# Linear attention and two token mixers on one core: attention products grouped by kind, buffers handed over by the program, one mixing in float32, a new order

## The chip, the core and the metric

The kernel runs on one core of a Trainium2 chip. The core has a matrix engine (TensorE, PE in the rows; its weight loads are shown as PEld), a vector engine (VectorE, DVE), a scalar engine (ScalarE, ACT), a general engine (GpSimd, POOL), and a queue that issues transfers (SyncE, SP). PE writes only into PSUM, which is used here as 8 banks of 128x512 float32. The metric is the device time of one execution in microseconds: 698.87 us before (median of 3 runs, 698.83 to 698.91).

## The reference

Three stages follow each other. Batch is 4, 768 tokens, 8 heads of 48 channels (384 channels in all).

```
# 1. linear attention with a decaying state, per batch and head
state = alpha[t, :, None] * state + outer(k[t], v[t]);   y[t] = q[t] @ state
# 2. first mixer: tokens through rank 32, then channels through 4*384
u  = x + (x.T @ U @ V).T;   x1 = u + relu(u @ w_ch1) @ w_ch2
# 3. second mixer
theta = x1 @ w_theta;  zr, zi = x1*cos(theta), x1*sin(theta)
u  = x1 + w_tok_r @ zr + w_tok_i @ zi;   out = u + relu(u @ w_ch)
```

## The kernel before

**Attention.** A pair of heads (64 partitions each, 48 used) of one batch is one unit of work; there are 16 such pairs, 4 to a batch. The 768 tokens are cut into 6 chunks of 128. `prep_k` and `prep_q` (L189 on, with `scale_k` and `scale_q` from L173 on) run two scans over the decay on VectorE (tiles `G` and `al`) and scale `kk` and `qq` by them; the multiplications are VectorE's for the first pairs and GpSimd's after that, as the strings `BY_K` and `BY_Q` say. `att_pe` (L217) then issues the products of a pair on TensorE, in kinds:

- `kT` (L248): five transposes of `kk`, copied by ScalarE into `kt`.
- `A` (L228): scores of a token half (three chunks, two heads). Each half is masked into two `Am` tiles: for the first four pairs by a copy on ScalarE and a select on GpSimd (L235, L236), for the others by a masked copy on VectorE (L239).
- `D` (L265): what each chunk adds to the state; two of its twelve products multiply zeros. A scan on VectorE (L272, tile `S`) turns it into states.
- `Y`: per half, the product of the masked scores with v (L285) and then that of the states with q (L290), into one bank; ScalarE copies it to `xp` (L292), and transfers carry it into the `X` tiles.

The order within a pair is: `kT`, `A` of half 0, `D`, scan, `A` of half 1, then for each half `Y` of the scores and `Y` of the states. In the trace a float32 product shows as two matmul instructions, so the 6 products of one `A` half are "x12".

**First mixer.** For batch 0, `rank_columns` (L342) works by 128 channels as soon as these are complete: transposes of `X` (L348), a split into a high and a low part (ScalarE L138, VectorE L139), 12 products with U in the reduced format fp32r (L308), and `lift` (L333), which multiplies by V (L335), adds to `X` on VectorE (L337) and splits the sum into `uh`. `expand` and `contract` are the channel products, 9 fp32r products of 384 columns each (L446 to L448), with weights that VectorE puts together from raw bits (`conv`, L376 to L380) and splits (L394). **Second mixer:** `theta`, `mix` (L600) and `chan`, all with such fp32r products.

**What sets the order.** The string `ORDER` names, letter by letter, the generator that is to issue its next piece (A attention, P preparation, D loads, 0 to 2 mixing of batch 0, L weights, M and N the channel products of the two token halves, and so on). Instructions keep that order on each engine. Tiles come from two pools: one tag of 59 slots in SBUF, one of 8 banks in PSUM; the pool gives a slot again when its tile is released.

Of the kernel before, what the change touches and what calls it, by code (L numbers as in the profile page):

```python
# [18 lines left out]
NP = H // 2  # L19
# [10 lines left out]


# [4 lines left out]
AAAPAAQAPAUAUAAUUPAAUAAAPUAAPAAAU00AALLDA0PAQALALALPLA10LAP0A1AAALL1LALAA212AQA22120LAMMLL21MLLLMLM1LLLMNNDMNM  # L36
MLMANLLNLNPNNLMMLLLMLNMLNMMQLLLLLNNMLMMLMMMDMPMPNAAQAQAAADPANAAPAAAAAAPLANAAADAAQPAANQADPNPNKKNNKKKKAAAAAAAPKK
KNAAKKNKQNADAAAAAPNMAAPMMMMQMKMMMMDPQMAAAAAAPQMMDMMAKMMAKMAAAAAAPMPNMNQMNDAMKAMKAAA2APAAMKANKPNNKKNDNKPQNNKNKA
NKAAAAAADPQNNNTPAANKNAAAAAAAPANAAAATAATAKNKMMKMMKMMMMNNKNNNKQMKKNKTNTMMMKMMTQKNNNNLMMMKMKUTNTLKLNNNNNNXMTMKTMT
NNMNMAHNNMKNKKNNHKHTKTNMNNMHHMNMMHMNNTMNLNMMTTNNFMMMMMTMMTTMNMHT0MNHTNNTTTMNTLNMMHNNMNMGTGHTHTNNHHTNHNTNGTGNNX  # L40
TNGTTGHTHHGTTGLTGGGLHGGGHGTGGXGHHGTTHAGHGGGHGGTTTTGGGPTGHHGGGHGHLGHGGGGFGGGGGFCGGHCCGHHHLHGFGDGHHGHMGGHGCGCGGH
NGHGGGGGPGTHHGGGHGGGGHCGGGHHCCGPGGHHHHGGGGHGGLGGHHGHGHGXGGGHHHGHGLG0GGHHGGGGHGCGHCGCHGGHGGGGCGHHGHGGGHGHGGGHGG
HHGGGGHHGHHGLLHGGGGGCGHGCGGGGCHLGGGCGGFGGGGCCCCCCCHCGC
# [4 lines left out]
    "VVVVPPPPPPPPPPPP", "VVVVPPPPPPPPPPPP", "VVVVVVVVVVVV",  # L48
# [12 lines left out]
def linear_attention_moe_kernel(ctx, tc, aT, kT, qT, vP, vT, U, V4, w1, w2, wth, wtr, wti, wch, out):  # L61
# [29 lines left out]

    def T(name, dt=F32):
        return pools["big"].tile([128, 768], dt, tag="s", name=name)

    def PS(name):
        return pools["ps"].tile([128, 512], F32, tag="p", name=name)
# [102 lines left out]
    def prep_q(b, p):  # L199
        if b + p:  # L200
            scale_q(b, p, 0, S)
        a, k, q, v, G = pr.pop((b, p))
        i = b * NP + p
        tt = pools["sml"].tile([128, NC, 1], F32, tag="tt", name="tt")
        tb = pools["sml"].tile([128, D, NC], F32, tag="tb", name="tb", bufs=2)
        dve.tensor_tensor(out=tt[:, 0:NC - 1], in0=v[:, NC * 96 + 1:NC * 97].unsqueeze(2), in1=cols(G, 0)[:, 1:NC],
                          op=ALU.mult)
        dve.memset(tt[:, NC - 1:NC], 0.0)  # L208
        act.copy(tb, tt.rearrange("p c o -> p o c").to_broadcast([128, D, NC]))
# [5 lines left out]
        pr[b, p] = (k, q, v, tb, squares)  # L215

    def att_pe(b, p):  # L217
        k, q, v, tb, squares = pr.pop((b, p))
# [3 lines left out]
        def scores(g):  # L222
# [7 lines left out]
            for h in range(2):  # L230
# [7 lines left out]
                else:  # L238
                    dve.copy_predicated(out=m, mask=maskb, data=t)  # L239
                ms.append(m)  # L240
            return ms

        def across(g):
# [5 lines left out]
            act.copy(k3[:, 3 * g:3 * g + n], t[:, 0:n * 128].rearrange("p (c d) -> p c d", d=128))  # L249

        across(0)
        if b + p:
            across(1)
        yield 750
        ma = scores(0)
        if b + p == 0:
            across(1)
        yield 1280
        late.append(squares)
        dps = PS("D")  # L260
        d3 = dps[:, 0:NC * D].rearrange("p (e c) -> p c e", c=NC)
        for c in range(NC):
            for h in range(2):
                w = v[:, c * 96 + h * D:c * 96 + (h + 1) * D] if c < NC - 1 else zero
                pe.matmul(d3[64 * h:64 * h + 64, c], k3[:, min(c, NC - 2), 64 * h:64 * h + 64], w,  # L265
                          start=True, stop=True)
        yield 800


        st = pools["sml"].tile([128, D, NC], F32, tag="S", name="S", bufs=2)  # L270
        flat = "p e c -> p (e c)"
        dve.tensor_tensor_scan(out=st.rearrange(flat), data0=dps[:, 0:NC * D], data1=tb.rearrange(flat),  # L272
                               initial=0.0, op0=ALU.add, op1=ALU.mult)
        yield
        mb = scores(1)
        yield 1280
        xp = T("xp")
        ms = (ma, mb)
        for g in range(2):
            t = PS("Y")  # L280
            cs = [(3 * g + j, slice(j * C, (j + 1) * C), j) for j in range(3)]
            for c, o, j in cs:
# [4 lines left out]
            for c, o, j in cs:  # L287
# [5 lines left out]
            yield 1500  # L293
        for h in range(2):
            ch = (2 * p + h) * D
            done = 0
            while done < D:
                j, r = divmod(ch + done, 128)
                n = min(D - done, 128 - r)
                sync.dma_start(X[b][j][r:r + n, :], xp[64 * h + done:64 * h + done + n, :])  # L300
                done += n
        yield 100
# [7 lines left out]
    def rank(b):  # L310
        g = PS("g")
        xs = {}
        for s in range(NC + 2):
            if s < NC:
# [4 lines left out]
                split(t[:, 0:384], xs[s][:, 0], xs[s][:, 1])  # L319
            if s > 1:  # L320
                x = xs.pop(s - 2)
                contract_tokens(g[:, 0:384], s - 2, x[:, 0], x[:, 1])
            yield 700
        gt = pools["sml"].tile([128, 384], F32R, tag="gt", name="gt", bufs=1)
        act.copy(gt, g[:, 0:384])
        dve.tensor_tensor(out=gt[96:128], in0=g[96:128, 0:384], in1=gt[96:128].bitcast(F32), op=ALU.subtract)
        yield
        for hf in range(2):
            for j in range(KD):
                lift(b, hf, j, gt[:, j * 128:(j + 1) * 128])  # L330
                yield

    def lift(b, hf, j, g):  # L333
        t = PS("h")
        pe.matmul(t[:, 0:HT], g, uv[1][:, hf * HT:(hf + 1) * HT], start=True, stop=True)  # L335
        x = X[b][j][:, hf * HT:(hf + 1) * HT]
        dve.tensor_tensor(out=x, in0=t[:, 0:HT], in1=x, op=ALU.add)  # L337
        uh = two(T("uh", F32R))
        split(x, uh[:, 0], uh[:, 1], e_hi=act)
        UH[b, hf, j] = uh  # L340

    def rank_columns(b, j):  # L342
        xs = []
        for n in range(2):
# [9 lines left out]
        for n in range(2):  # L354
            for i in range(3):
                s = 3 * n + i
                o = slice(i * 128, (i + 1) * 128)
                contract_tokens(g[:, 0:128], s, xs[n][:, 0, o], xs[n][:, 1, o])
# [3 lines left out]
        dve.tensor_tensor(out=gt[96:128], in0=g[96:128, 0:128], in1=gt[96:128].bitcast(F32), op=ALU.subtract)  # L362
        yield
# [20 lines left out]
    def load_w12():  # L384
# [3 lines left out]
        def put(n, W):  # L388
            def high(v):
# [3 lines left out]
                def low():  # L393
                    (dve if BY_W[n] == "V" else pool).tensor_tensor(out=l, in0=v, in1=h.bitcast(F32), op=ALU.subtract)  # L394
                    W.extend((two(h)[:, i], two(l)[:, i]) for i in range(2))
# [29 lines left out]
    def load_uv():  # L425
# [9 lines left out]
        pool.tensor_tensor(out=a[:, :, 0:RANK], in0=u3, in1=a[:, :, RANK:2 * RANK].bitcast(F32), op=ALU.subtract)  # L435
        v4 = T("v4", F32R)
        act.copy(v4, got[1])
        pool.tensor_tensor(out=v4[32:64], in0=got[1][32:64], in1=v4[32:64].bitcast(F32), op=ALU.subtract)
        yield 0
        uv[:] = [a, v4]  # L440
# [10 lines left out]

    def expand(b, hf, f, uh, pend=pend):
        t = PS("h1")
        for j in range(KD):
# [5 lines left out]
                                 op0=ALU.max, op1=ALU.subtract)  # L460
        pend.append((b, hf, f, h))

    def contract(pend=pend):
# [3 lines left out]
        for j in range(KD):  # L467
            w = [x[:, j * 128:(j + 1) * 128] for x in W2[f]]
            three(acc[b, hf][j][:, 0:HT], w, (h[:, 0], h[:, 1]), f == 0, f == NF - 1)
        if f == NF - 1:  # L470
            for j, t in enumerate(acc.pop((b, hf))):
                x = X[b][j][:, hf * HT:(hf + 1) * HT]
                dve.tensor_tensor(out=x, in0=t[:, 0:HT], in1=x, op=ALU.add)
            ended.append(b)
# [25 lines left out]
    def spill(b):  # L500
        for j in range(KD):
            d = dr.tile([128, 768], F32, name=f"x1d{b}_{j}")
            sync.dma_start(d, X[b][j])
            x1d[b, j] = d
# [5 lines left out]
    def load_second():  # L510
# [3 lines left out]
        def put_thch(v):  # L514
            v = two(v)
            pool.tensor_scalar(out=v[:, 0], in0=v[:, 0], scalar1=INV2PI, scalar2=0.0, op0=ALU.mult, op1=ALU.add)
            for i, W in ((0, TH), (1, CH)):
                t = two(T("wt", F32R))
                split(v[:, i], t[:, 0], t[:, 1], e_lo=by())
                W.append(t)  # L520

# [407 lines left out]
```

## Time and profile before

| | |
|---|---|
| median of 3 runs | 698.87 us |
| profiled execution | 698.41 us, span of its instructions 696.7 us |
| PE busy | 670.8 us (96%), 4818 instructions |
| DVE, ACT, POOL busy | 397.7 (57%), 248.1 (36%), 139.6 (20%) us |
| granted TensorE clock, mean | 0.995 |
| chain of waits | 85% of the span on PE, 6% DVE, 3% issue, 2% DMA, 2% POOL |

The page's busy share is an average over stages. Up to 63.07 us, where the channel products of the first mixer begin, PE has gaps and DVE is the busiest engine; from there to 691.11 us, its last product, PE hardly stops; the last 5.6 us are the final vector operations and the transfers of the result.

### The profile page before, as it was taken

The page shows a single profiled execution, that of the slowest core. Times are in us where ns is not written, and L with a number is a line of the kernel's source. Part 1 is how long each engine was busy: PE and PEld are TensorE (multiplying, and loading weights), DVE is VectorE, ACT ScalarE, POOL GpSimd, SP SyncE. Part 2 cuts the span into 40 slices and gives each one's busy share as a digit, 9 for nine tenths or more (in the row PEclk, how much of TensorE's full clock was granted, in tenths as well). Part 3 has the DMA queues.
Part 4 walks back from the last instruction along what each step waited for, and adds up shares of the span by engine and source line. Part 5 has one row for each costly group of instructions (what it writes and reads, how often), then busy time and mean ns, then how long its engine had stood idle before and what let it go on. Part 6 is the DMA issues. An engine that isn't in the chain of part 4 may idle for free.

```text
span 696.7 us, 11660 instructions
## 1 busy us (share of the span) xinstructions
PE 670.8 (96%) x4818; PEld 640.9 (92%) x4818; DVE 397.7 (57%) x610; ACT 248.1 (36%) x512; POOL 139.6 (20%) x123
## 2 busy tenths in 40 slices
PE   5879999999999999999999999999999999999996
PEld 4658999898888998899999999999999999999996
DVE  7798887686545565435344635667644363344423
ACT  3554332454332433324233323234343243434310
POOL 5440011431321231001121111323440121112010
PEclk9999999999999999999999999999999999999999
DMA  8562656163712233102120311244100000000012
GB/s 311 178 227 64 221 165 193 40 195 103 250 50 78 86 103 109 36 1 113 56 104 1 114 45 47 91 159 158 47 1 35 24 13 22 1 35 12 1 45 97
DMA packets 24078, 63.22 MB, mean 91 GB/s; under 512 B 2896, under 2 KB 6864, under 8 KB 24016
## 3 DMA queue, kind: packets, MB, share of 16 engines
q1 hardware_dynamic: 24016, 62.39, 26.6%
q8 instruction: 40, 0.66, 0.4%
q14 instruction: 22, 0.18, 0.1%
HBM read 49.40 MB, written 8.26 MB: 83 GB/s over the span
## 4 chain that ended last, share of the span: by engine, by line
PE 85%; DVE 6%; issue 3%; DMA 2%; POOL 2%; ACT 1%; SPq 1%; POOLq 0%; ACTq 0%; DVEq 0%
PE mx L600 19%; PE h L446 7%; PE acc L446 7%; PE acc L447 7%; PE h L448 7%; PE h L447 7%; PE acc L448 7%; PE A L228 3%; PE Y L285 3%; PE Y L290 3%; PE ch L448 2%; PE ch L447 2%; PE ch L446 2%; PE th L448 2%; PE th L447 2%
## 5 line engine op out<-in xcount | busy, mean ns | idle before, releaser
L459 DVE SCALAR_TENSOR_TENSOR hh<-h,hh 128x384 fp32r<-128x384 f32 x96 | 52.4, 554 | 103.2 <-ACT hh L458 103.2
L447 PE MATMUL acc<-hh,wh 128*128 128x384 f32 x288 | 96.5, 335 | 1.4 <-DVE hh L459 1.4
L446 PE MATMUL h<-uh,wh 128*128 128x384 f32 x288 | 97.7, 339 | 0.1
L446 PE MATMUL acc<-hh,wh 128*128 128x384 f32 x288 | 97.5, 339 | 0.0
L448 PE MATMUL acc<-hh,wl 128*128 128x384 f32 x288 | 96.5, 335 | 0.0
L448 PE MATMUL h<-uh,wl 128*128 128x384 f32 x288 | 96.5, 335 | 0.0
L447 PE MATMUL h<-uh,wh 128*128 128x384 f32 x288 | 96.4, 335 | 0.0
L458 ACT ACTIVATE hh<-h 128x384 fp32r<-128x384 f32 x96 | 46.0, 489 | 97.2 <-PE h L448 93.3
L600 PE MATMUL mx<-wkh,zh 128*128 128x384 f32 x288 | 74.8, 340 | 0.0
L600 PE MATMUL mx<-wkl,zh 128*128 128x384 f32 x288 | 73.3, 335 | 0.0
L600 PE MATMUL mx<-wkh,zl 128*128 128x384 f32 x288 | 73.2, 335 | 0.0
L447 PEld LDWEIGHTS acc<-hh,wh 128*128 128x128 f32 x288 | 54.1, 188 | 1.7 <-DVE hh L459 1.7
L446 PEld LDWEIGHTS h<-uh,wh 128*128 128x128 f32 x288 | 54.1, 188 | 1.6 <-DVE hh L459 0.7
L446 PEld LDWEIGHTS acc<-hh,wh 128*128 128x128 f32 x288 | 54.1, 188 | 1.1
L448 PEld LDWEIGHTS acc<-hh,wl 128*128 128x128 f32 x288 | 54.1, 188 | 0.1
L447 PEld LDWEIGHTS h<-uh,wh 128*128 128x128 f32 x288 | 54.1, 188 | 0.0
L448 PEld LDWEIGHTS h<-uh,wl 128*128 128x128 f32 x288 | 54.1, 188 | 0.0
L600 PEld LDWEIGHTS mx<-wkh,zl 128*128 128x128 f32 x288 | 52.1, 188 | 0.0
L600 PEld LDWEIGHTS mx<-wkl,zh 128*128 128x128 f32 x288 | 51.9, 188 | 0.0
L600 PEld LDWEIGHTS mx<-wkh,zh 128*128 128x128 f32 x288 | 50.9, 188 | 0.0
L139 POOL TENSOR_TENSOR wkl<-cv,wkh 128x768 fp32r<-128x768 f32 x12 | 22.8, 1901 | 100.4 <-ACT wkh L138 100.4
L187 POOL TENSOR_TENSOR qq<-qq,al 128x768 f32<-128x768 f32 x12 | 23.4, 1952 | 92.4 <-DVE tt L208 50.2
(126 smaller groups left out, 1193.1 us busy)
## 6 DMA issues: line engine op xcount, KB each, us to landing
raw<-in_w SPq DMA_DIRECT2D x12, 768.0 KB, 4.5
al<-in_aT SPq DMA_DIRECT2D x15, 384.0 KB, 3.8
kk<-in_kT SPq DMA_DIRECT2D x15, 384.0 KB, 4.7
qq<-in_qT SPq DMA_DIRECT2D x15, 384.0 KB, 5.1
vv<-in_vP SPq DMA_DIRECT2D x16, 291.0 KB, 5.4
raw<-in_wtr SPq DMA_DIRECT2D x6, 768.0 KB, 4.2
raw<-in_wti SPq DMA_DIRECT2D x6, 768.0 KB, 4.2
out<-ot SPq DMA_DIRECT2D x24, 192.0 KB, 1.9
```

The source lines that it names most:

```text
L139: (e_lo or dve).tensor_tensor(out=lo, in0=src, in1=hi.bitcast(F32), op=ALU.subtract)
L187: (dve if BY_Q[b * NP + p] == "V" else pool).tensor_tensor(out=q[:, o], in0=q[:, o], in1=a[:, o], op=ALU.mult)
L228: pe.matmul(ts[h][:, j * C:(j + 1) * C], k[r, c], q[r, c], start=True, stop=True)
L285: pe.matmul(t[64 * h:64 * h + n, o], v[:, c * 96 + h * D:c * 96 + h * D + n], ms[g][h][:, j], start=(j == 0), stop=(c == 0), skip_group_ch ...
L290: pe.matmul(t[64 * h:64 * h + D, o], st[64 * h:64 * h + 64, :, c - 1], q[64 * h:64 * h + 64, c * C:(c + 1) * C], start=False, stop=True, s ...
L446: pe.matmul(out, a[0], b[0], start=first, stop=False)
L447: pe.matmul(out, a[0], b[1], start=False, stop=False)
L448: pe.matmul(out, a[1], b[0], start=False, stop=last)
L458: act.activation(h[:, 0], t[:, 0:HT], ACTF.Relu)
L459: dve.scalar_tensor_tensor(out=h[:, 1], in0=t[:, 0:HT], scalar=0.0, in1=h[:, 0].bitcast(F32), op0=ALU.max, op1=ALU.subtract)
L600: pe.matmul(ACC[b, j][hf][:, 0:HT], z[:, i, c], w[:, hf * HT:(hf + 1) * HT], start=f, stop=l)
```

## The change

1. `att_pe` with `LATE = 0` issues both halves of a kind together: `kT`, `A` of half 0, `A` of half 1, `D`, the scan, `Y` of the scores for both halves, `Y` of the states for both halves.
2. `D` leaves out its two products with zeros; VectorE writes the zeros into the bank before the scan.
3. Tiles are taken from lists of free slots and banks that the program keeps itself (`take`, `done_with`); each slot has a tag of its own, and the slot that was given back first is taken first.
4. For batch 0 `rank_columns` mixes in float32: `xs` is one plain copy, six products with a float32 tile `uf` take the place of twelve with `ua`. In `lift` (batch 0), a product of the identity with `X` adds `X` in the bank, ScalarE copies the sum back, and the split reads the bank.
5. One pair's `qq` multiplication goes from GpSimd to VectorE (`BY_Q`), squares are noted earlier, X tiles are allocated when first written, and `ORDER` is another string.

```
+LATE = 0
...
-    "VVVVPPPPPPPPPPPP", "VVVVPPPPPPPPPPPP", "VVVVVVVVVVVV",
+    "VVVVPPPPPPPPPPPP", "VVVVPPPVPPPPPPPP", "VVVVVVVVVVVV",
...
+    free, home = {"on": True, "s": list(range(SLOTS)), "p": list(range(8))}, {}
+    def take(kind, name, width, dt):
+        p = pools["big" if kind == "s" else "ps"]
+        if not free["on"]:
+            return p.tile([128, width], dt, tag=kind, name=name)
+        i = free[kind].pop(0)
+        t = p.tile([128, width], dt, tag=f"{kind}{i}", name=name, bufs=1)
+        home[t.tensor.name] = kind, i
+        return t
...
+    def done_with(*ts):
+        for t in ts:
+            if t.tensor.name in home:
+                kind, i = home.pop(t.tensor.name)
+                free[kind].append(i)
...
+        def increments():
+            t = PS("D")
+            d3 = t[:, 0:NC * D].rearrange("p (e c) -> p c e", c=NC)
+            for c in range(NC - 1 if after else NC):
...
+        def states(t):
+            if after:
+                dve.memset(t[:, 0:NC * D].rearrange("p (e c) -> p c e", c=NC)[:, NC - 1], 0.0)
...
+        after = b * NP + p >= LATE
+        across(0)
...
+        ms.append(scores(0))
...
+        if after:
+            yield
+            ms.append(scores(1))
+            done_with(k)
+            yield
+            dps = increments()
+            yield
+            st = states(dps)
+            yield
+            xp = T("xp")
+            ts = [PS("Y") for _ in range(2)]
+            for g in range(2):
+                within(ts[g], g)
...
+            yield
+            for g in range(2):
+                before(ts[g], g)
...
     def lift(b, hf, j, g):
         t = PS("h")
...
+        if b == 0:
+            pe.matmul(t[:, 0:HT], ident, x, start=True, stop=False)
+            pe.matmul(t[:, 0:HT], g, uv[1][:, hf * HT:(hf + 1) * HT], start=False, stop=True)
+            split(t[:, 0:HT], uh[:, 0], uh[:, 1], e_hi=act)
+            act.copy(x, t[:, 0:HT])
+            done_with(t)
+            return
...
     def rank_columns(b, j):
...
-            x = two(T("xs", F32R))
-            split(t[:, 0:384], x[:, 0], x[:, 1])
-            xs.append(x)
+            act.copy(two(xs)[:, n], t[:, 0:384])
...
-                contract_tokens(g[:, 0:128], s, xs[n][:, 0, o], xs[n][:, 1, o])
+            pe.matmul(g[:, 0:128], uv[2][:, o], xs[:, o], start=(s == 0), stop=(s == NC - 1))
...
+        w = T("uf")
+        pool.memset(w, 0.0)
+        act.copy(w.rearrange("p (s n r) -> p s n r", s=NC, n=4)[:, :, 1:4], u3.unsqueeze(2).to_broadcast([128, NC, 3, RANK]))
```

Three places show how instructions stand. First PE, the pair after the first batch (the sixth row of `kT` in the program before): one kind per token half.

```order
L248 MATMUL kT<-ident,kk 128x128 x5
L228 MATMUL A<-qq,kk 128x128 x6
L265 MATMUL D<-vv,kt 64x48 x10
L265 MATMUL D<-zero,kt 64x48 x2
L228 MATMUL A<-qq,kk 128x128 x6
L285 MATMUL Y<-Am_84,vv 64x128
L285 MATMUL Y<-Am_84,vv 48x128
...
L290 MATMUL Y<-qq,S 48x128 x4
L285 MATMUL Y<-Am_85,vv 64x128
L285 MATMUL Y<-Am_85,vv 48x128
...
L290 MATMUL Y<-qq,S 48x128 x6
```

The same pair in the changed program, on PE:

```order
L273 MATMUL kT<-ident,kk 128x128 x5
L252 MATMUL A<-qq,kk 128x128 x12
L284 MATMUL D<-vv,kt 64x48 x10
L305 MATMUL Y<-Am_84,vv 64x128
L305 MATMUL Y<-Am_84,vv 48x128
...
L305 MATMUL Y<-Am_85,vv 64x128
L305 MATMUL Y<-Am_85,vv 48x128
...
L313 MATMUL Y<-qq,S 48x128 x10
```

The second half of `A` has moved ahead of `D`, the two `Y` products of scores stand together, and those of states too.

Second, DVE while pair 4 is prepared in the start of the program before. (`xs` and `uh` are splits of the mixing, `gc` the mixed rank, `cv` and `wl` a weight, the others attention.)

```order
L272 SCALAR_TENSOR_TENSOR S<-D,tb 128x288
L139 TENSOR_TENSOR xs<-xt,xs 128x384
L362 TENSOR_TENSOR gc<-g,gc 32x128
L394 TENSOR_TENSOR wl<-cv,wh 128x768
L380 SCALAR_TENSOR_TENSOR cv<-raw,cv 128x768
L185 RECIPROCAL starts<-G 128x6
L186 SCALAR_TENSOR_TENSOR al<-al,starts 128x768
L206 TENSOR_TENSOR tt<-vv,G 128x5
L208 MEMSET tt 128x1
L337 TENSOR_TENSOR X_160<-h,X_160 128x384
L139 TENSOR_TENSOR uh<-X_160,uh 128x384
L139 TENSOR_TENSOR xs<-xt,xs 128x384
```

The same preparation in the changed program, on DVE:

```order
L292 MEMSET D 128x48
L295 SCALAR_TENSOR_TENSOR S<-D,tb 128x288
L449 TENSOR_TENSOR gc<-g,gc 32x128
L205 RECIPROCAL starts<-G 128x6
L206 SCALAR_TENSOR_TENSOR al<-al,starts 128x768
L226 TENSOR_TENSOR tt<-vv,G 128x5
L228 MEMSET tt 128x1
L466 TENSOR_SCALAR cv<-raw 128x768
L468 SCALAR_TENSOR_TENSOR cv<-raw,cv 128x768
L449 TENSOR_TENSOR gc<-g,gc 32x128
L159 TENSOR_TENSOR uh<-h,uh 128x384
L484 TENSOR_TENSOR wl<-cv,wh 128x768
```

The splits `xs` and the addition to `X` are gone from DVE, a short memset has come, and the first `wl` stands later.

Third, PE in the start of the changed program, where the float32 mixing of batch 0 meets pair 4:

```order
L444 MATMUL g<-xs,uf 128x128 x6
L273 MATMUL kT<-ident,kk 128x128 x5
L420 MATMUL h<-X_243,ident 128x384
L421 MATMUL h<-v_400,gc 128x384
L252 MATMUL A<-qq,kk 128x128 x12
L284 MATMUL D<-vv,kt 64x48 x10
L437 MATMUL xt<-ident,X_472 128x128 x6
L420 MATMUL h<-X_243,ident 128x384
L421 MATMUL h<-v_400,gc 128x384
L420 MATMUL h<-X_336,ident 128x384
L421 MATMUL h<-v_400,gc 128x384
L444 MATMUL g<-xs,uf 128x128 x6
```

Before, a mixing product `g` was twelve fp32r products, and `h` one product (L335) without L420.

## Rows read from the trace of the kernel before

**Rows 1.** The page, part 1: busy time, share of the span, instructions.

```profile
PE 670.8 (96%) x4818; PEld 640.9 (92%) x4818; DVE 397.7 (57%) x610; ACT 248.1 (36%) x512; POOL 139.6 (20%) x123
```

**Rows 2.** Stretches: length; busy PE, PEld, DVE, ACT, POOL; clock; DMA share, GB/s.

```profile
0.00:63.07 63.07, 46.72 (x543) 36.83 (x543) 54.09 (x80) 30.51 (x70) 24.42 (x40) 0.97 0.61 215
13.83:64.17 50.34, 41.67 (x500) 33.02 (x499) 44.30 (x67) 27.89 (x64) 17.71 (x18) 0.97 0.54 191
63.07:691.11 628.04, 624.09 (x4277) 604.04 (x4275) 343.02 (x529) 217.62 (x443) 115.16 (x83) 1.00 0.24 78
```

**Rows 3.** Waits of PE up to 63 us: total, times, longest.

```profile
PE kT L248 <- DVE starts L185: 5.0, 1, 5.0
PE Y L285 <- POOL Am L236: 3.8, 3, 2.2
```

**Rows 4.** Waits of PE from 63 to 691 us.

```profile
PE A L228 <- POOL qq L187: 2.0, 2, 1.0
```

**Rows 5.** PE in order of time, one pair: start, length, what.

```profile
157.63 0.79 PE L265 MATMUL D<-vv,kt 128*64 128x48 f32 x20
158.25 0.29 PE L265 MATMUL D<-zero,kt 128*64 128x48 f32 x4
158.46 0.94 PE L228 MATMUL A<-qq,kk 64*128 64x128 f32 x12
159.33 0.87 PE L285 MATMUL Y<-Am,vv 128*64 128x128 f32 x12
160.13 0.68 PE L290 MATMUL Y<-qq,S 64*48 64x128 f32 x8
160.74 0.87 PE L285 MATMUL Y<-Am,vv 128*64 128x128 f32 x12
161.54 0.90 PE L290 MATMUL Y<-qq,S 64*48 64x128 f32 x12
162.37 0.97 PE L308 MATMUL g<-xs,ua 128*128 128x384 f32 x4
```

**Rows 6.** PE in order of time, a mixing product of batch 0.

```profile
58.97 1.24 PE L308 MATMUL g<-xs,ua 128*128 128x128 f32 x12
60.05 0.39 PE L335 MATMUL h<-v,gc 128*128 128x384 f32 x1
```

**Rows 7.** Groups by line and shape: busy us, mean ns, idle before.

```profile
L139 DVE TENSOR_TENSOR xs<-xt,xs 128x384 fp32r<-128x384 f32 x24 | 12.9, 549 | 7.6 <-ACT xs L138 7.5
L337 DVE TENSOR_TENSOR X<-h,X 128x384 f32<-128x384 f32 x24 | 13.2, 550 | 4.3 <-PE h L335 4.1
L394 DVE TENSOR_TENSOR wl<-cv,wh 128x768 fp32r<-128x768 f32 x12 | 11.9, 994 | 0.0
L380 DVE SCALAR_TENSOR_TENSOR cv<-raw,cv 128x768 int32<-128x768 int32 x28 | 30.5, 1091 | 0.4
L376 DVE TENSOR_SCALAR cv<-raw 128x768 int32<-128x768 int32 x28 | 19.9, 709 | 2.8 <-DMA raw<-in_w 2.8
L186 DVE TENSOR_TENSOR_SCAN al<-al,starts 128x768 f32<-128x768 f32 x15 | 28.9, 1924 | 0.7
L335 PE MATMUL h<-v,gt 128*128 128x384 f32 x18 | 6.1, 358 | 0.0
L208 DVE MEMSET tt<- 128x1 f32 x16 | 0.9, 59 | 0.0
L362 DVE TENSOR_TENSOR gc<-g,gc 32x128 fp32r<-32x128 f32 x3 | 0.9, 297 | 0.1
```

**Rows 8.** POOL in order of time, two selects each.

```profile
21.29 0.99 POOL L236 TENSOR_SCALAR_AFFINE_SELECT Am<-Am 128x384 f32<-128x384 f32 x2 [4.00 <-ACT Am L235]
22.99 2.52 POOL L236 TENSOR_SCALAR_AFFINE_SELECT Am<-Am 128x384 f32<-128x384 f32 x2 [0.71 <-ACT Am L235]
```

**Rows 9.** ACT in order of time: the last copy of pair 1's result.

```profile
27.30 0.48 ACT L292 COPY xp<-Y 112x384 f32<-112x384 f32 x1 [2.98 <-PE Y L290]
```

**Rows 10.** PE in order of time: the first transposes of `X`.

```profile
30.58 0.84 PE L348 MATMUL xt<-ident,X 128*128 128x128 f32 x6 [0.93 <-DMA X<-xp]
```

More of the change, by code (lines that the diff above doesn't have):

```diff
@@ L208, in prep_q @@
         dve.memset(tt[:, NC - 1:NC], 0.0)
+        if i == B * NP - 1:
+            done_with(starts, ends)
         act.copy(tb, tt.rearrange("p c o -> p o c").to_broadcast([128, D, NC]))
@@ L249, in across @@
             act.copy(k3[:, 3 * g:3 * g + n], t[:, 0:n * 128].rearrange("p (c d) -> p c d", d=128))
[L251 to L282, printed above, removed]
+            done_with(t)
@@ new lines, in increments @@
+        def increments():
+            t = PS("D")
+            d3 = t[:, 0:NC * D].rearrange("p (e c) -> p c e", c=NC)
+            for c in range(NC - 1 if after else NC):
+                for h in range(2):
+                    w = v[:, c * 96 + h * D:c * 96 + (h + 1) * D] if c < NC - 1 else zero
+                    pe.matmul(d3[64 * h:64 * h + 64, c], k3[:, min(c, NC - 2), 64 * h:64 * h + 64], w,
+                              start=True, stop=True)
+            done_with(kt)
+            return t
@@ new lines, in states, with within @@
+        def states(t):
+            if after:
+                dve.memset(t[:, 0:NC * D].rearrange("p (e c) -> p c e", c=NC)[:, NC - 1], 0.0)
+            s = pools["sml"].tile([128, D, NC], F32, tag="S", name="S", bufs=2)
+            flat = "p e c -> p (e c)"
+            dve.tensor_tensor_scan(out=s.rearrange(flat), data0=t[:, 0:NC * D], data1=tb.rearrange(flat),
+                                   initial=0.0, op0=ALU.add, op1=ALU.mult)
+            done_with(t)
+            return s
+        def within(t, g):
+            for j in range(3):
+                c, o = 3 * g + j, slice(j * C, (j + 1) * C)
@@ L286, in att_pe, with before @@
                               start=(j == 0), stop=(c == 0), skip_group_check=True)
-            for c, o, j in cs:
+        def before(t, g):
+            for j in range(3):
+                c, o = 3 * g + j, slice(j * C, (j + 1) * C)
                 for h in range(2):
@@ L292, in att_pe @@
             act.copy(xp[0:112, g * 384:(g + 1) * 384], t[0:112, 0:384])
-            yield 1500
+            done_with(t)
+        ms = []
+        after = b * NP + p >= LATE
+        across(0)
+        if b + p:
+            across(1)
+        yield
+        ms.append(scores(0))
+        if b + p == 0:
+            across(1)
+        if after:
[11 more added lines that the diff above has]
+                within(ts[g], g)
+            done_with(v)
+            if b * NP + p == B * NP - 1:
+                done_with(*Am[::2])
+            yield
+            for g in range(2):
+                before(ts[g], g)
+            done_with(q)
+            yield
+        else:
+            yield
+            dps = increments()
+            yield
+            st = states(dps)
+            yield
+            ms.append(scores(1))
+            done_with(k)
+            yield
+            xp = T("xp")
+            for g in range(2):
+                t = PS("Y")
+                within(t, g)
+                before(t, g)
+                if g:
+                    done_with(v, q)
+                yield
         for h in range(2):
@@ L322, in rank @@
                 contract_tokens(g[:, 0:384], s - 2, x[:, 0], x[:, 1])
+                done_with(x)
+            if s == NC + 1 and b == B - 1:
+                done_with(uv[0])
             yield 700
@@ L625, in mix @@
                         U2[b, hf, j] = ts[hf]
-        for s in range(NC):
-            Z.pop((b, s))
         for j in range(KD):
@@ L651, in chan @@
                                          op0=ALU.max, op1=ALU.add)
+                done_with(t)
                 sync.dma_start(dst(e)[:, hf * HT:(hf + 1) * HT], ot)
+                if e == KD - 1:
+                    done_with(*us)
                 yield 1450
+        done_with(*[X[b][j] for j in range(KD)])
         del X[b]
@@ L696, in linear_attention_moe_kernel @@
     more_constants()
-    X[0] = [T(f"X{j}") for j in range(KD)]
     oks = cst.tile([128, B * NP * 2], F32, name="oks")
@@ L740, in products @@
             if x[0] not in X:
-                X[x[0]] = [T(f"X{j}") for j in range(KD)]
+                X[x[0]] = {}
             for step, _ in enumerate(att_pe(*x)):
@@ L749, in squared @@
             while not late:
-                next(gens["A"], None)
+                next(gens["P"], None)
             late.pop(0)()
@@ L840, in linear_attention_moe_kernel @@
     fast.close()
+    free["on"] = False
     with tc.If(fine[0] < 1):
```

90 lines of the change are left out of this document (69 added, 21 removed).

## The prediction, made before the changed kernel ran

> **What bounds the kernel now.** I read the page's busy shares first: PE is busy for 670.8 of 696.7 us [rows 1], so the time is PE's work plus the time in which PE waits. The stretches show where the waiting is [rows 2]. Up to 63.07 us PE is busy for 46.72 us and VectorE (DVE) for 54.09; from there to PE's last product at 691.11 us PE is busy for 624.09 of 628.04. So there are two regimes. In the start, up to the first channel product, DVE's chain sets the pace. After it PE does, and there every microsecond of PE work that goes is one off the end, unless a new wait takes it. The list of PE's waits agrees: in the start it waits for VectorE's first scans (5.0 us) and GpSimd's selects (3.8) [rows 3]; after it the largest sum is 2.0 us, in two waits, for GpSimd's `qq` [rows 4]. A third look, at one pair in order of time, gives the price of each kind of product, from one group's start to the next one's [rows 5].
>
> **The change part by part.**
>
> *Both halves of a kind together, zeros off PE.* In rows 5 `D` takes 0.83 us to the start of `A` (157.63 to 158.46), a half of `A` 0.87, a half of `Y` from scores 0.80, `Y` from states 0.61 with 8 instructions and 0.83 with 12. Four instructions more thus cost 0.22 us, 0.055 each, and the rest of a group is what starting it costs. I use 0.055 for all kinds with 128 columns. Both halves of `A` as one group: 0.87 + 12 x 0.055 = 1.53 in place of 1.74 (0.21 less). `Y` from scores: 0.80 + 0.66 = 1.46 for 1.60 (0.14 less). `Y` from states: 0.83 + 8 x 0.055 = 1.27 for 1.44 (0.17 less). `D` without its four zero instructions: 20 of them take 0.62 us, 0.031 each, so 0.12 less. Together 0.64 us a pair. Pairs 0 to 4 lie in the start, where PE isn't the bound; pairs 5 to 15 are 11 x 0.64 = 7.0 us off PE's path.
>
> The order binds these kinds closer than before, so what PE waits for has to be early enough. In a pair without other work between, the masks of the first half can start 0.9 us after `A` starts and all four are done some 2.1 us later; `A` and `D` last 1.53 + 0.71 = 2.24, the first half of `Y` 0.8 more. The scan comes behind the fourth mask and `D`, and `Y` from scores (1.46 us) covers it. That is just even, so I charge nothing, and a rival below takes up what happens when VectorE comes late. Its memset of 128x48 in the bank is not shown: the nearest rows are 0.06 us (a memset of one column) and 0.30 (an operation out of a bank on 32 partitions) [rows 7]; I take 0.1.
>
> *Float32 mixing of batch 0.* Twelve reduced products took 1.08 us (58.97 to 60.05) [rows 6]. Six float32 products are twelve instructions over the whole array. The instructions of rows 5 cover half of the array (64*128, 128*64), and I take two to run side by side at 0.11 a pair, so one that fills it takes 0.11: 1.32 us, 0.24 more, three times, all in the start. The product of the identity with `X` has 384 columns: 3 x 0.11 x 2 instructions = 0.66 us. Its lower end is the reduced product of the same shape, 0.36 [rows 7]; I take 0.66, since the other float32 products are nearer than a reduced one. By the Trainium skill ("FP8 and Floating Point Precision", TensorE Precision Notes) a true float32 product makes four passes through the array, which speaks for the upper end; no row shows such a product filling the array. Of the six, the new order leaves two behind the first channel product, with the 20 instructions of pair 4's `Y` from states: 2 x 0.66 + 1.27 = 2.6 us that PE now does after the start (two lifts stood behind it before as well).
>
> *The start.* DVE was busy for 44.30 us from 13.83, after the first state scan, to 64.17, when the third split `uh` that the channel products need was done, and waited for 6.0 [rows 2]. Of this go six `xs` splits (6 x 0.55), three additions to `X` (3 x 0.55), and, moved behind the start by the new order, one `wl` (0.99) and two steps of a weight's conversion (1.09 and 0.71) [rows 7]; one `uh` more (0.6) and four memsets (0.4) come in. 44.3 - 3.3 - 1.65 - 2.8 + 1.0 = 37.6 us. What DVE waits for changes. `D` of pair 1 now stands behind both halves of `A`: pair 0 ends on PE at about 19.4, then `kT`, `A` and `D` (0.64 + 1.53 + 0.72) end at 22.3, while DVE is there after two scans, two multiplications and some conversion at 20.7: 1.7 us. `D` of pair 2 stands behind the transposes of `X`, which need pair 1's result to have been stored; from its last copy to the transposes it was 3.3 us (27.30 to 30.58) [rows 9, 10], so `D` ends near 33.3 and DVE waits for 1.5. The mixing of pair 4's time, through ACT casts and PE lifts back to DVE, I put at 3.1, as the copies that free the bank stand in ACT's queue between them. With 0.2 for a later first scan that is 6.5 us of waits. The third `uh` comes at 13.8 + 37.6 + 6.5 = 57.9 and a little for PE's lift of that column, 58.3, in place of 64.17: 5.9 us earlier. The moved conversions then lie beside PE's channel products, where DVE was busy for 343.02 of 628.04 us [rows 2]. The bounds: no waits at all, 12.5 us earlier; twice the waits, none.
>
> *The rest at nothing.* Plain copies on ACT take the place of casts of the same size; the copy of `X` and the float32 `uf` (a memset on GpSimd, a copy on ACT) add some 4 us to an engine that was busy for 30.51 of 63.07 [rows 2]. The hand-over of slots and banks frees in the order of the program as the pools did; the number of waits in the program is nearly the same, so I give it 0, and +-2 us for a load that starts sooner or later. One `qq` on VectorE falls to pair 7, where PE has channel products between the pairs.
>
> *Sum.* -7.0 + 2.6 - 5.9 = -10.3. The profiled execution took 698.41 us, 1.7 over its span, and the median of the runs is 0.46 higher: 698.87 - 10.3 = 688.6, say 688.5 us.
>
> **The rivals.**
>
> *The start gains more.* DVE finds all inputs ready: 12.5 in place of 5.9, 682.0 us. For it: DVE's order has shorter work ahead of each state scan. Against it: three of its inputs come from PE, later than before.
>
> *The start gains little, held by GpSimd's selects.* For pairs 0 to 3 all four masks now come one behind the other. Two selects took 0.99 us in one place and 2.52 in another, where a VectorE scan ran beside them [rows 8]. If one more pair of selects of each of pairs 1 to 3 is slow, 3 x 1.53 = 4.6 us of the 5.9 are gone, 693.2 us. The Trainium skill ("SBUF — State Buffer", Who interferes with whom) says that a VectorE instruction with two SBUF inputs and a GpSimd one that reads SBUF exclude each other for the whole instruction; by that rule the selects wait for scans each time and this rival holds. For it: the scans are most of DVE's work there. Against it: DVE stands still while it waits for `D`, as the selects run.
>
> *Slower: VectorE comes late to every pair.* In a pair without other work, `Y` waits for masks and scan that stand in DVE's queue behind one `al` scan of 1.92 us [rows 7] of the next pair's preparation. Before, the second half of `A` and its own masks gave the scan more room. Eleven pairs at 1.92 are 21.1 us: 709.6. It decides from 10.3 / 11 = 0.94 us a pair. Against it: in the order, the next pair's scans come behind this pair's state scan, and two channel groups of PE lie between pairs.
>
> *No change.* The selects hold the start and each pair waits for about 0.5 us: 698.7.
>
> **How the numbers follow.** Forecast 0.50, start gains more 0.13, start gains little 0.22, no change 0.06, slower 0.09. What a measurement of this kernel can tell from no change is 0.2%, 1.4 us. The first three are faster: 0.85; same 0.06; slower 0.09. The forecast's own range is 685 to 692 (identity products at 0.36 take 0.6 us off; hand-over 2 either way; half the waits' error). Reaching to the first two rivals and a little beyond: 681 to 697.
>
> **What would show it.** In the changed profile the first channel product should start at 57 to 58 us, not 63. A pair after the start should show `A` as one group of 24 instructions, 1.5 us to the next group, and `Y` of 24 and 20 at 1.46 and 1.27. L420 should show 12 instructions, 0.66 us for two. DVE should have no `X` addition or `xs` split for batch 0. From the first channel product to PE's last it should be about 628 - 4.4 = 624 us. I am wrong if PE's waits after the start sum to more than 10 us, with `S` or `Am` of VectorE as releaser, or if the first channel product starts after 62 us.

## The result, and the profile after

The changed kernel takes 682.66 us (median of 4 runs, 682.56 to 683.93) against 698.89: a ratio of 0.9771, 95% interval 0.9759 to 0.9783, 16.2 us less. 688.5 was forecast, with a range of 681 to 697; the narrower range given with it, 685 to 692, was missed. The direction and the mechanism of the pairs held; the gain was half as large again as forecast. The time lies beside the 682.0 us of the rival *The start gains more*, but that rival wanted 12.5 us from the start, which gave 6.4. The page of the profile after, part 1, answers to [rows 1]:

```profile
PE 661.6 (97%) x4766; PEld 638.4 (94%) x4766; DVE 396.9 (58%) x615; ACT 250.5 (37%) x519; POOL 143.5 (21%) x123
```

The stretches answer to [rows 2]: the start up to the first channel product, DVE from behind the first state scan to the end of the third split `uh`, and the rest up to PE's last product. The columns are length; busy PE, PEld, DVE, ACT, POOL; clock; DMA share, GB/s.

```profile
0.00:56.67 56.67, 43.75 (x511) 35.26 (x512) 51.07 (x74) 27.67 (x64) 26.14 (x41) 1.00 0.64 226
13.84:57.94 44.10, 37.81 (x463) 30.65 (x459) 41.65 (x58) 22.90 (x55) 19.28 (x18) 1.00 0.56 196
56.67:675.22 618.55, 617.84 (x4256) 603.14 (x4255) 345.28 (x541) 222.84 (x455) 117.39 (x82) 1.00 0.25 81
```

The first channel product starts at 56.67 in place of 63.07 us, 6.4 earlier, and PE then needs 618.55 in place of 628.04, 9.5 less. The span is 15.9 shorter; the tail behind PE's last product is the same. One pair after the start, PE in order of time, answers to [rows 5]:

```profile
117.75 0.71 PE L273 MATMUL kT<-ident,kk 128*128 128x128 f32 x5
118.39 1.61 PE L252 MATMUL A<-qq,kk 64*128 64x128 f32 x24
119.93 0.79 PE L284 MATMUL D<-vv,kt 128*64 128x48 f32 x20
120.54 1.73 PE L305 MATMUL Y<-Am,vv 128*64 128x128 f32 x24
122.32 1.34 PE L313 MATMUL Y<-qq,S 64*48 64x128 f32 x20
123.59 0.45 PE L542 MATMUL acc<-hh,wh 128*128 128x384 f32 x1
```

From start to start `A` takes 1.54 us, `D` 0.61, `Y` from scores 1.78, `Y` from states 1.27. Three of the four are about what was worked out (1.53, 0.71, 1.46, 1.27) or less; `Y` from scores is 0.3 longer, and DVE at the same time shows why:

```profile
119.36 2.01 DVE L263 COPY_PREDICATED Am<-mask,A 128x384 f32<-128x384 int32 x4 [0.85 <-PE A L252]
121.38 0.10 DVE L292 MEMSET D<- 128x48 f32 x1
121.51 0.76 DVE L295 TENSOR_TENSOR_SCAN S<-D,tb 128x288 f32<-128x288 f32 x1
```

Four masks, memset and scan stand in one queue and end at 122.27; the products of the states start 0.05 later. Where nothing makes them late they start 1.42 us behind those of the scores (in 2 of 11 pairs), here 1.78. PE loses 0.36 us, 0.24 of it in the second half of the group, whose masks come then, and 0.11 at `S`; because the products before are still running the list of waits hardly counts it. The whole stretch, as sums of the distances from each product's start to the next one's, in us:

| from the first channel product on | before | after |
|---|---|---|
| `kT` | 9.08 | 6.04 |
| `A` | 19.64 | 17.63 |
| `D` | 9.19 | 6.80 |
| `Y` from scores | 18.87 | 18.14 |
| `Y` from states (11 pairs, then 12) | 15.86 | 15.20 |
| lifts with the identity products | 4.01 | 5.50 |
| channel and mixer products (3023 in both) | 532.65 | 530.42 |
| transposes, rank mixing, flag | 18.42 | 18.49 |
| sum | 627.72 | 618.22 |

### The profile page after: what moved, and what is told of

It reads as the page before. It is cut to its first block, busy times and chain, and to the rows that moved or that the text cites. A ratio compares the mean times of both kernels' runs of the same rounds, so it can differ in the third digit from the quotient of the medians.

```text
span 680.8 us, 11581 instructions
## 1 busy us (share of the span) xinstructions
PE 661.6 (97%) x4766; PEld 638.4 (94%) x4766; DVE 396.9 (58%) x615; ACT 250.5 (37%) x519; POOL 143.5 (21%) x123
## 4 chain that ended last, share of the span: by engine, by line
PE 91%; DVE 5%; DMA 1%; issue 1%; POOL 1%; ACT 1%; SPq 0%; DVEq 0%; ACTq 0%; POOLq 0%
PE mx L724 22%; PE acc L542 8%; PE h L542 7%; PE acc L544 7%; PE acc L543 7%; PE h L543 7%; PE h L544 7%; PE Y L313 3%; PE A L252 3%; PE Y L305 3%; PE th L544 2%; PE ch L542 2%; PE ch L544 2%; PE th L542 2%; PE th L543 2%; PE ch L543 2%
## 5 line engine op out<-in xcount | busy, mean ns | idle before, releaser
L199 POOL TENSOR_TENSOR kk<-kk,G 128x767 f32<-128x767 f32 x12 | 21.9, 1829 | 111.4 <-DVE G L197 87.5
L691 ACT COPY xc<-x1t 128x384 f32<-128x384 f32 x24 | 11.5, 479 | 82.2 <-PE x1t L685 82.2
```

The costliest lines, as they stand in the source:

```text
L199: (dve if BY_K[b * NP + p] == "V" else pool).tensor_tensor(out=k[:, x:y - 1], in0=k[:, x:y - 1], in1=G[:, x:y - 1], op=ALU.mult)
L691: act.copy(xc, xt[:, 0:DM])
```

## The experiments

The first four cross the code with the order. E1, E3, E4 and E5 leave the hand-over of slots and banks to the pools; E1 shows what that alone is worth.

**E1: hand-over by the pools.**

```
-    free, home = {"on": True, "s": ...
+    free, home = {"on": False, "s": ...
```

> The changed kernel, but slots and banks are handed over by the pools as before. Theory A (the hand-over is worth nothing; of the 16.2 us, 6.4 are the start, some 5 the shorter PE work after it and some 4.5 are waits of PE after the start that the new order took away): within 1.4 us of the changed kernel, 681.3 to 684.1. Theory B (the surplus over the forecast, 5.9 us, is the hand-over's, since loads and copies start sooner with a slot that was given back first): about 688, at least 685.

682.60 us; first channel product at 56.55, 618.2 us behind it. Theory A: the hand-over is worth nothing.

**E2: the new order with the old code** (the `ORDER` string is the only edit to the kernel before).

> The kernel before, with the changed kernel's ORDER string and nothing else of the change. Theory A (the new order alone takes away the waits of PE after the start, 4 to 4.5 us, and moves 2.8 us of conversions behind the start): 691 to 694. Rival C (the order only works with kinds put together and the lighter mixing; with the old code it makes VectorE late in other places): 698 or more. PE's waits after the first channel product should be 1 us or less by A (about 4.6 before), 4 or more by C.

721.21 us, 22.3 slower than before, with a first channel product at 68.72. The string is the same, but not all of the order that comes of it. The letter `Q` notes squares; where none are ready, the program before lets attention issue pieces until some are (`squared`, L747), and the changed program turns to preparation instead. From the first channel product to 238 us PE's groups stand as in E4 (below), which has the new code. Then one `Q` pulls four pieces, and `kT`, `A` and `D` of pair 13 come 36 to 81 channel products earlier than in E4. PE's waits from 69 to 240 us, and after:

```profile
PE acc L448 <- DVE wl L394: 1.3, 1, 1.3
PE Y L290 <- DVE S L272: 0.3, 1, 0.3
```

```profile
PE h L446 <- DVE hh L459: 5.6, 1, 5.6
PE A L228 <- POOL qq L187: 5.6, 2, 4.7
...
```

The first long one stands at the place that `Q` moved:

```profile
242.01 0.71 PE L248 MATMUL kT<-ident,kk 128*128 128x128 f32 x5
247.41 1.65 PE L228 MATMUL A<-qq,kk 64*128 64x128 f32 x12 [4.69 <-POOL qq L187]
```

By its time this is rival C's case. But up to 238 us theory A had it right: the two waits of [rows 4] (before `A` of pairs 6 and 12) are gone with the old code too, `kT` to `A` is 0.64 us in both. PE ends 21.5 us later than in E4, and 17.8 of these come behind `kT` of pair 12 (233.76 us). The granted clock was 0.50 for 34 us in all, 13.7 of them behind 240 us (for 3.4 us in the first 63 us of the kernel before).

**E3: the old order with the new code** (the `ORDER` string of before in the changed kernel, E1's edit too).

> The changed kernel with the ORDER string of the kernel before (slots and banks by the pools, since the old order needs more of them alive). Theory A (parts add up: waits of 4 to 4.5 us come back, and the conversions stand in the start again, 2 to 3 us): 688 to 690. Rival C (code and order only work together): 693 or more. Theory D (the order is worth nothing, the waits went with the kinds): 683 to 685.

705.30 us, 6.4 slower than before, with a first channel product at 65.45:

```profile
PE xt L391 <- DMA X<-xp: 5.4, 1, 5.4
...
PE D L284 <- DVE hh L564: 2.3, 2, 1.7
PE Y L313 <- DVE S L295: 2.1, 1, 2.1
...
```

By its time rival C again. Here too a part of the order is another: where `Q` pulled attention forward in the kernel before, it does not now. `A` and `D` of pair 10 come 9 channel products later than there, `kT` of pairs 11 to 13 comes 54 to 81 later, and the wait of 5.4 us (at 241.78) stands behind that. Neither the code nor the order gained anything without the other here, but only up to 195 us (E3) and 238 us (E2), the start included, are the two runs clean crossings.

**E4: token halves in every pair, new order.**

```
-LATE = 0
+LATE = 16
```

> The changed kernel with LATE = 16: every pair goes by token halves again, with the two products of zeros on PE (slots and banks by the pools). Theory A: the groups after the start give back what they gained, 2.3 (A) + 2.4 (D) + 1.5 (Y from scores) + 1.9 (Y from states) less the 2.3 us that Y from states now waits for the scan: 687.5 to 690. Rival D (the grouping also took the 4.5 us of waits away, since masks and scans come earlier in the pair): 692 to 695. The first channel product stays at 56 to 57.5 us by A; by a rival in which grouping shortens the start it comes 2 us later or more.

699.45 us. Behind the first channel product PE needs 624.7 us, 6.5 more, as theory A had it, and its waits there do not come back: the list has one of 0.3 us for `S`. But the first channel product comes at 67.13, 10.5 later, as in the rival named there without a price, in which grouping shortens the start. PE's waits up to there, those of the changed kernel up to its own, and ScalarE and GpSimd around the longest but one:

```profile
PE Y L305 <- POOL Am L260: 8.7, 5, 3.6
...
```

```profile
...
PE Y L305 <- POOL Am L260: 2.6, 5, 0.9
...
```

```profile
33.70 0.83 ACT L532 CAST v<-cv 128x768 fp32r<-128x768 f32 x1
34.44 0.85 ACT L438 COPY xs<-xt 128x384 f32<-128x384 f32 x2
35.18 0.87 ACT L259 COPY Am<-A 128x384 f32<-128x384 f32 x2
```

```profile
34.68 2.00 POOL L533 TENSOR_TENSOR v<-cv,v 32x768 fp32r<-32x768 f32 x1 [1.59 <-ACT v L532]
36.75 0.99 POOL L260 TENSOR_SCALAR_AFFINE_SELECT Am<-Am 128x384 f32<-128x384 f32 x2
```

With halves, the second half's masks are issued later and stand behind a weight's cast `v` and the copies `xs` in both queues; `Y` starts at 37.32 after a wait of 2.9 us. With both halves together all four masks are issued ahead of these.

**E5: halves in the five pairs of the start alone** (E1's edit too).

```
-LATE = 0
+LATE = 5
```

> The changed kernel with LATE = 5: the five pairs of the start go by token halves, the eleven later ones by kinds (slots and banks by the pools, which alone change nothing). Theory A (halves in the start put the second masks behind other work in ScalarE's and GpSimd's queues, which makes the start 10.5 us longer; kinds in the later pairs are worth 6.5 us): first channel product at 67 us, 692 to 694.5 in all. Rival B (the 10.5 us are a property of all sixteen pairs together, or are made up later where PE has slack): 685 to 690.

694.27 us, first channel product at 68.68, 618.4 us behind it (618.2 after). The same wait as in E4 (8.9 us in five places, 8.7 there). Theory A held: kinds together are worth 6.2 to 6.5 us in the eleven late pairs and more than that in the five of the start. Up to the first channel product E4 and E5 are the same program; the 1.55 us between them go with the granted clock, which was 0.50 for 13.6 us of E5's start and for 6.8 us of E4's, and never in the start of the changed kernel's profile.

**E6: batch 0 mixed in the reduced format, new order.**

```
-            act.copy(two(xs)[:, n], t[:, 0:384])
+            split(t[:, 0:384], x[:, 0], x[:, 1])
...
-            pe.matmul(g[:, 0:128], uv[2][:, o], xs[:, o], start=(s == 0), stop=(s == NC - 1))
+                contract_tokens(g[:, 0:128], s, xs[n][:, 0, o], xs[n][:, 1, o])
...
-        if b == 0:
+        if False:
```

> The changed kernel with batch 0 mixed in the reduced format as before (xs split on ScalarE and VectorE, twelve products, X added by VectorE). Theory A, the prediction's (VectorE's work bounds the start: 6 xs splits and 3 additions to X, 4.95 us, come back): first channel product at 60 to 62 us; PE behind it saves two identity products and their switches, 1.2; 685.5 to 688. Rival B (the start is bound by masks, GpSimd's selects and transfers; VectorE has room since the conversions moved): first channel product at 56 to 58, 681 to 683.5.

692.67 us, first channel product at 63.87: more than theory A's 60 to 62. Behind it PE needs 620.7 us, 2.4 more in place of 1.2 less; it waits 2.3 us there for a weight's split `wl`. DVE, then PE, then ScalarE:

```profile
31.55 1.02 DVE L159 TENSOR_TENSOR xs<-xt,xs 128x384 fp32r<-128x384 f32 x2 [4.41 <-ACT xs L158]
```

```profile
36.65 2.38 PE L313 MATMUL Y<-qq,S 64*48 64x128 f32 x20 [7.27 <-DVE S L295]
```

```profile
29.74 0.67 ACT L533 COPY uf<-cv 128x576 f32<-128x576 f32 x1 [2.12 <-POOL uf L532]
```

The split is not only work. It waits 4.41 us for ScalarE's cast, and the next `G`, `kk` and the scan `S` that PE needs stand behind it in DVE's queue; `Y` from states starts here at 36.65, 31.45 in the changed kernel. Some of this wait is the experiment's own: the float32 tile `uf` is still made though nothing reads it, and its copy stands ahead of the cast in ScalarE's queue and waited 2.12 us for GpSimd's memset. The granted clock was 0.50 for 13.6 us of this start, so the 7.2 us are an upper bound of what the mixing is worth.

**E7: the zeros on PE again, no memset.**

```
-            for c in range(NC - 1 if after else NC):
+            for c in range(NC):
...
-            if after:
-                dve.memset(...)
```

> The changed kernel with the two products of zeros in D back on PE and no memset by VectorE. By the rows D takes 0.835 us with them and 0.62 without. Theory A (all of it is on PE's path in eleven pairs): 11 x 0.21 = 2.4 us slower, 684.5 to 685.5. Rival B (Y from states waits for the scan anyway, 2.3 us in sum over ten pairs, and the scan comes 0.1 earlier without the memset, while masks are the last thing it waits for; so PE's extra 0.21 us only takes the place of a wait): 682.5 to 683.5.

682.15 us, no difference (its profiled run took 684.33, the others 681.79 to 682.31). `D` gets 1.3 us longer, `A` 1.2 (1.1 of it in one pair, where ScalarE's copy `kt` comes late), and `Y` from scores 2.1 shorter: rival B. In the pair shown above it is 3.82 us from `A` to `Y` from states, 3.93 with the memset: masks, memset and scan set this time, not PE's four instructions.

**E8: a channel-product piece between `A` and `D`** (eight pairs; one place in `ORDER`):

```
-...MPMAAAAQDAUAQPANPAUNAAA...
+...MPMAAANAQDAUAQPAPAUNAAA...
```

> The changed kernel with one letter of ORDER moved in each of eight pairs (5 to 8, 11 to 14): the next channel-product piece stands between A and D, not behind Y. Theory A (Y from states waits for the scan, 0.1 to 0.37 us a pair, 2.3 in sum, and D waits for kT's copy, 0.5 in sum; both go, and a switch between formats costs 8 x 0.09): 2 us faster, 680 to 681.5. Rival B (the waits move to the channel products, whose hh is not ready that early): 682.5 or more.

685.78 us. `Y` from scores falls to 1.42 us in five of the spaced pairs and to 1.51 to 1.57 in three, 16.24 in all (18.14 after): the wait for `S` is real and goes. But `kT` grows from 6.04 to 9.29 and the channel products by 1.3. PE's waits behind the first channel product:

```profile
PE A L252 <- POOL qq L207: 3.0, 2, 1.6
PE A L252 <- DVE hh L564: 0.5, 1, 0.5
```

The next pair's `A` now finds GpSimd's `qq` late. Theory A was right on `S` and wrong on the sum; rival B named the wrong place.

**E9: E8 with the `qq` of pairs 6 and 9 on VectorE** (`BY_Q` "VVVVPPVVPVPPPPPP").

> The kernel of the spaced order (a channel-product piece between A and D in eight pairs, 685.7) with the qq multiplications of pairs 6 and 9 on VectorE as well, where A had waited 1.40 and 1.56 us for GpSimd's qq. Theory A (those waits are what the spacing cost): they go, 682.2 to 683.2, and no A waits over 0.6 us after the start. Rival B (VectorE's queue takes the wait over: masks, scans or hh come later by 1 us each): 684.5 or more.

685.19 us. The waits are taken over by DVE's and ScalarE's queues:

```profile
PE A L252 <- DVE tt L228: 0.7, 1, 0.7
PE A L252 <- DVE hh L564: 0.5, 1, 0.5
PE A L252 <- ACT kt L274: 0.3, 1, 0.3
```

Rival B. No version tried here is faster than the changed kernel by more than the runs scatter.

**E10: X added by VectorE, mixing still in float32** (`if b == 0:` in `lift` becomes `if False:`).

> The changed kernel with the mixing still in float32, but X added by VectorE in batch 0 (no product with the identity; the split reads X). Theory A (the identity product is not free: two lifts behind the first channel product took 1.72 us with it, and without it some 0.5; in the start VectorE gets 3 x 0.55 and a step more of latency per lift, which move the first channel product by 1.5 to 3 us): first channel product at 58 to 60, time behind it 617.0 to 617.3, 682.8 to 685. Rival B (in the start VectorE has room for it): first channel product at 56.3 to 57.2, 681 to 682.

688.04 us: first channel product at 58.86, 2.2 later (theory A), and 622.3 us behind it, which neither had. DVE is now so late that a weight is too, and after this wait the clock falls. PE's wait, then the stretches around it:

```profile
PE acc L544 <- DVE wl L484: 2.4, 1, 2.4
```

```profile
69.56:70.80 1.24, 1.24 (x6) 1.24 (x7) 1.24 (x2) 0.34 (x1) 0.00 (x0) 0.91 0.74 292
70.80:73.70 2.90, 2.90 (x10) 2.90 (x10) 2.87 (x5) 0.89 (x2) 0.00 (x0) 0.50 0.73 215
```

**E11: pair 7's `qq` on GpSimd** (`BY_Q` as before).

> The changed kernel with pair 7's qq on GpSimd again. Theory A, the prediction's (worth nothing, GpSimd is idle for 7 us before that pair): 682 to 683.4. Rival B (the qq comes behind others in GpSimd's queue and the pair's A waits for it as pair 6's and 10's did before the change): 1 to 2 us slower, 683.6 to 684.8.

682.71 us: theory A, nothing. The start of its profile had 3.4 us at a granted clock of 0.50, that of the changed kernel none; its first channel product came at 56.78, 0.1 later, so such a stretch need not cost the start what it costs PE.

**E12: two of pair 2's masks by VectorE.**

```
-    "AAAAAAAAVVVVVVVVVVVVVVVVVVVVVVVV", "PPPPPPPPPPPPPPP",
+    "AAAAAVAAVVVVVVVVVVVVVVVVVVVVVVVV", "PPPPPPPPPPPPPPP",
```

> The changed kernel with the masks of pair 2's second half made by VectorE (two copies of 0.5 us) in place of ScalarE and GpSimd, whose selects PE waits for there (0.90 and 0.76 us). Theory A (VectorE's chain bounds the start, GpSimd's selects only fill its time): first channel product 0.5 to 1.2 us later, 57.2 to 57.9, 683 to 684. Rival B (the selects bound it): first channel product 0.8 to 2 us earlier, 680.5 to 682.

684.12 us, first channel product at 58.40. PE:

```profile
34.20 2.37 PE L313 MATMUL Y<-qq,S 64*48 64x128 f32 x20 [4.89 <-DVE S L295]
```

The waits for selects are gone there and a longer one for VectorE's scan has come: theory A, a little stronger than expected. `Y` from states starts 2.75 us later here than in the changed kernel (31.45), where DVE's chain bounds the start: beside the two masks, its `kk` took 2.37 us next to GpSimd's `v` (1.09 in the changed kernel). The granted clock was 0.50 for 6.8 us from 32.2 us on.

## Why the prediction was right, and where it was wrong

*The pairs after the start: right.* -7.0 was forecast. `A` gave 2.0, `D` 2.4, `Y` from scores 0.7, and `Y` from states 1.9 (0.7 in the table, and a twelfth group of 1.27 beside it): 7.1. E4 and E5 show 6.2 to 6.5 for it directly. Two errors inside cancel. `D` fell by 0.22 us a pair, not 0.12; with the zeros back it takes 0.73 (E7), so they are 0.11 of it, and the rest is that `Y` now follows and not `A`. And "just even, so I charge nothing" was too kind: `Y` from scores takes 1.42 us where nothing makes the next kind late and 18.14 / 11 = 1.65 on the mean, so waiting for DVE costs 11 x 0.23 = 2.5 us. That is the mechanism of the rival on the slower side at an eighth of its price, 0.23 a pair for 1.92.

*Behind the start: right.* 2.6 us was forecast for two lifts and pair 4's `Y` from states; the lifts cost 1.5 more than before and the `Y` 1.27: 2.8. But not as thought. The rows that answer to [rows 6], PE in order of time:

```profile
60.02 0.81 PE L420 MATMUL h<-X,ident 128*128 128x384 f32 x2
60.37 0.63 PE L421 MATMUL h<-v,gc 128*128 128x384 f32 x1
60.83 0.81 PE L420 MATMUL h<-X,ident 128*128 128x384 f32 x2
61.18 0.63 PE L421 MATMUL h<-v,gc 128*128 128x384 f32 x1
61.74 1.34 PE L313 MATMUL Y<-qq,S 64*48 64x128 f32 x20
```

The identity product takes 0.35 us, the lower of the two ends; the step that failed is "0.66 us for two". The rest comes from going back to float32 behind the reduced product, 0.46 and 0.56 us where a reduced one goes on after 0.18. By the Trainium skill ("FP8 and Floating Point Precision", TensorE Precision Notes) true float32 makes four passes; here a float32 product of this shape took 0.35 us and a reduced one 0.173, two to one, and the measurement decides.

*The start: the size was right, the account of it was not.* The third split ended 44.1 us behind the scan, as forecast (37.6 of work and 6.5 of waits). It is 41.65 of work and some 2.4 of waits. The waits for `D` of pairs 1 and 2 did not come; DVE reached both scans behind other work. And three of DVE's instructions became 4.0 us longer beside GpSimd (last section).

The step that failed is "Pairs 0 to 4 lie in the start, where PE isn't the bound", by which kinds together counted for nothing there. With the new order they are worth 10.5 us (E4; 12.0 in E5 at a lower clock), since they decide when the masks of the second half enter ScalarE's and GpSimd's queues: PE's waits for selects are 8.7 us in E4 and 2.6 after. The clock that fell in E4 is at most some 3 us of the rest (an estimate: 6.8 us at the spacing of 0.32 in place of 0.173 us that the last section shows for E10); what else is in it was not separated. The relief of DVE that I took for the whole gain is worth at most 7.2 us of start under the new order (E6), in part as a wait that goes. Under the old order both together bring the first channel product 2.4 us later (E3). The terms of a start in which four engines wait for each other do not add up, and mine agreed with the measured 6.4 partly by luck. The rival that lets GpSimd's selects hold the start had its condition, since four of them took 2.82 to 4.82 us where two can take 0.99; yet PE waited for them 2.6 us in place of 3.8 [rows 3], and with two fewer the start got longer (E12).

*The surplus, 5.9 us.* The start gave 0.5 more, pairs and lifts together 0.1 less, and 0.3 lie between the profiled runs and the medians. The rest is in two rows of the table that I had at nothing: `kT`, 3.0, and channel products, 2.2. In `kT` lie the waits of [rows 4] for `qq`, 2.1 us from start to start; another 0.9 is mostly that `kT` is now followed by a reduced product (0.46 us) in six pairs, by `A` (0.64) in five; before it was two and nine. In the channel products of before there was one wait for `hh`, 1.6 us from start to start, in the list of PE's waits that [rows 4] begins; the other 0.6 is spread:

```profile
...
PE acc L447 <- DVE hh L459: 1.4, 1, 1.4
...
```

After, the list from 56 us on holds only these, with `gc` still in the start:

```profile
PE h L421 <- DVE gc L449: 0.5, 1, 0.5
PE Y L313 <- DVE S L295: 0.2, 1, 0.2
PE xt L391 <- DVE Am L263: 0.2, 1, 0.2
```

The failed step is that I read [rows 4] as "the largest sum is 2.0 us, in two waits" and then left these waits standing in the sum, as though a new order would keep the waits of the old one. The waits for `qq` are gone with token halves (E4), with the mixing in the reduced format (E6, `kT` 6.06) and, up to 238 us, with the old code (E2); with the old order and the new code one of them stands, 1.6 us before `A` of pair 6 (E3). So it is the order that takes them away.

*At nothing, and nothing:* the hand-over (E1) and pair 7's `qq` (E11). The zeros, which had a gain of 0.12 us a pair, are worth nothing as well (E7).

## What to carry to other kernels

Where an order is written out for one code, crossing the two prices neither unless the order that runs is the one meant: here the new code with the old string cost 6.4 us, the old code with the new string 22.3, and both gained 16.2, but one letter meant other work in either code, and most of the 22.3 came behind the place where it did. Compare the order of the products in the traces first. Price a regrouping in the start too, by what it moves ahead of what in each in-order queue, and list the waits of the old order as terms that may go. Look at the granted clock of each start that is compared, too. A group of products that shrinks on a busy engine gains only down to the chain of the engine that feeds the next group; look for a distance from start to start that is longer than the products, since the list of waits can miss it.

## What the runs showed of the hardware that was not expected

VectorE's longest surprises in the start stand beside a GpSimd instruction, VectorE first and GpSimd second:

```profile
33.91 1.77 DVE L226 TENSOR_TENSOR tt<-vv,G 128x5 f32<-128x5 f32 x1
...
42.29 2.63 DVE L206 TENSOR_TENSOR_SCAN al<-al,starts 128x768 f32<-128x768 f32 x1
...
44.90 0.55 DVE L466 TENSOR_SCALAR cv<-raw 128x768 int32<-128x768 int32 x1
...
45.49 2.46 DVE L468 SCALAR_TENSOR_TENSOR cv<-raw,cv 128x768 int32<-128x768 int32 x1
```

```profile
33.43 2.23 POOL L533 TENSOR_TENSOR v<-cv,v 32x768 fp32r<-32x768 f32 x1 [1.59 <-ACT v L532]
...
41.49 1.81 POOL L199 TENSOR_TENSOR kk<-kk,G 128x767 f32<-128x767 f32 x1
44.99 2.13 POOL L207 TENSOR_TENSOR qq<-qq,al 128x768 f32<-128x768 f32 x1 [1.69 <-DVE tt L228]
```

A product of 5 columns, 0.16 us elsewhere, took 1.77 and ended with GpSimd's `v`; the scan took 0.87 more than its 1.76, the conversion 1.5 more than its 0.96. By the Trainium skill ("SBUF — State Buffer", Who interferes with whom) a VectorE instruction with two inputs from SBUF and a GpSimd one that reads SBUF contend for a shared port pair, which is an exclusive lock, and one with at most one input is free of it, outside the modes that use both ports. For two inputs the trace agrees. The prediction cited this rule for GpSimd's selects alone; here it charged VectorE itself, 4.0 us.

The conversion step with one input (L466) shows no such freedom. At 44.90 it kept its 0.55 us, but it had begun 0.09 us before `qq`, and `qq` took 2.13 in place of 1.84. Later, begun 0.29 us behind GpSimd's `kk`, it took 1.97 and ended 0.42 behind it; VectorE first again:

```profile
97.74 1.97 DVE L466 TENSOR_SCALAR cv<-raw 128x768 int32<-128x768 int32 x1
```

```profile
97.45 1.84 POOL L199 TENSOR_TENSOR kk<-kk,G 128x767 f32<-128x767 f32 x1 [50.33 <-DVE G L197]
```

No run here shows in which mode it ran.

In E10 PE stood for 2.4 us, went on at 69.56, and in the stretch from 70.80 to 73.70 the granted clock was 0.50 (1.2 GHz), and channel products started 0.32 us apart in place of 0.173. Nine of them cost 1.3 us more, beside the wait.
